# Last token block of a gated attention and convolution mix projected group by group from SBUF, its last group of heads normalized by 32x32 transposes on VectorE

## The chip, the cores and the metric

The kernel runs on one core of a Trainium2 chip. The core has five engines with an instruction queue each: TensorE (PE; its weight loads are listed as PEld), VectorE (DVE), ScalarE (ACT), GpSimd (POOL) and SyncE (SP), which here mostly issues DMAs. PE multiplies tiles held in SBUF and writes to PSUM, which has eight banks of 512 float32 columns on 128 partitions. The metric is the device time of one execution in microseconds, as a median of several runs. One more execution was recorded by the hardware profiler; all rows of a profile are of that one.

## What is computed

One batch of S = 2048 tokens, D = 640 channels, in bfloat16. `x = A_q` feeds two branches, and a gate of each token mixes them:

```python
x = A_q
g = _sigmoid((x * gate_w).sum(-1, keepdims=True))
a = _A_ref(x, A_k, A_v, A_shift_k, A_ssm_k, A_ssm_D)   # short shift, long convolution, times q
b = _B_ref(x, B_wq, B_wk, B_wv, B_wo)                  # attention
return g * a + (1 - g) * b

# _B_ref: 32 heads of Dh = 20, one shared k and v (multi-query)
q = (x @ wq).reshape(B, S, 32, 20).transpose(0, 2, 1, 3)
k = x @ wk
v = x @ wv
p = _softmax(einsum("bhqd,bkd->bhqk", q, k) * 20 ** -0.5)
o = einsum("bhqk,bkd->bhqd", p, v)
b = o.transpose(0, 2, 1, 3).reshape(B, S, 640) @ wo
```

The change is in the last two lines of the attention branch: the division of the softmax by its sum, and the product with `wo`, for the last quarter of the tokens.

## The kernel before

The tokens are cut into four blocks of 512 (`NB = 4`, index I). The 32 heads are cut into eight groups of four (index g); a head takes 32 of the 128 partitions, of which 20 hold its channels. For one block and one group the kernel walks over 16 tiles of 128 keys (index j). So `attention` (L879) has 4 x 8 x 16 = 512 steps u, 128 to a block. A step is: four matmuls QK (L893) into four PSUM banks, two exponentials of 128x1024 on ScalarE (L909; two steps in sixteen have one of them done by VectorE instead, L923 to L931), and four matmuls PV (L935) that add into bank 6. `vaug` carries a column of ones at position 20, so that row 20 of each head's 32 rows in bank 6 is the sum of the exponentials.

After the sixteen steps of a group `norm` (L990) divides. It copies bank 6 to `acc` (L994). The four rows of sums go by DMA to a 128x16 tile `den`, VectorE takes the reciprocal (L998), a DMA stores it to DRAM (`scr_d`), a DMA reads it back spread over all partitions (`rbc`), VectorE multiplies (L1004) into `oTn`, and a DMA stores that to DRAM (`scr_o`).

When all eight groups of a block are in `scr_o`, `oproj` (L1196) loads them in another layout (`oTp`, five tiles of 128 channels without the gaps), by four DMAs, and projects: for each of four tiles of 128 tokens (ci) and two halves of 320 output columns, five matmuls (L1211) and one eviction on VectorE (L1214), which scales by 1 - g (`omgf`) and adds the convolution branch, `kv`. The tile `outsb` is then stored to the output. `load_wo` (L1220) loads `wo` in the matching layout.

The convolution branch (`conv`, L1065) has its matmuls on PE, its spectra on VectorE and its complex products on GpSimd; it runs beside the attention and ends before the last block does.

Every operation is a node of a graph with the tiles that it reads and writes as keys. The `Scheduler` (L133) plays the graph through with modelled costs and writes out one fixed order for each engine. Three of its rules matter here. Operations marked `main` (QK, the exponentials, PV) keep their order, and the other matmuls come in groups, each with a PSUM bank, that are put in gaps of the main order by priority. A bank that a main operation uses is claimed for good (`bank_claimed`), and no group may take it afterwards. Where PE has nothing else and has been busy less than half of the last 2.4 modelled microseconds, a filler matmul with zero weights goes into bank 6 (L1256 names where it is made; not between the last PV of a group and the first of the next). On the chip each engine follows its list in order, with semaphore waits where another engine's result is needed. DMAs use one of 40 lanes, each with a semaphore; at the end SP waits for every lane in turn (L434 and L435).

`alloc` (L539) lays out SBUF: `xT` (x transposed, 20 KB a partition) and `wq_pad` (10 KB) are last read by the query projection of the last block (L839). `fence` (L127) makes the first writer of a family of tiles wait for all users of the families that lay there before. L502 is the helper through which all DMAs go.

Of the kernel before, what the change touches and what calls it, by code (L numbers as in the profile page):

```python
# [7 lines left out]
ALU = mybir.AluOpType  # L8
AX = mybir.AxisListType

BF16 = dt.bfloat16
F32 = dt.float32
# [120 lines left out]
class Scheduler:  # L133
# [238 lines left out]
    def emit(self, nc):  # L372
        def ctr(o):
            return "d%d" % o.lane if o.kind == "d" else "c_" + o.eng

        for op in self.linear:
            drop = [d for d in op.deps if op.eng == "pe" and d.eng == "pe" and d.kind == "c"]
            for d in drop:
                op.deps.discard(d)
            for d in op.deps:  # L380
                d.sig = True
        for e in ENGS:
            n = 0
            for op in self.order[e]:
                if op.kind == "d":
                    op.sig = True
                elif op.sig:
                    n += 1
                    op.value = n
        known = {e: {} for e in ENGS}  # L390
        waits = {}
        for op in self.linear:
            kn = known[op.eng]
            need = {}
            for d in sorted(op.deps, key=lambda o: -(o.value or 0)):
                c = ctr(d)
                if kn.get(c, 0) >= d.value:
                    continue
                if need.get(c, (0, None))[0] < d.value:
                    need[c] = (d.value, d)  # L400
            final = []
            items = sorted(need.items(), key=lambda kv: -kv[1][1].end)
            for c, (v, d) in items:
                if kn.get(c, 0) >= v:
                    continue
                final.append((c, v))
                for kc, kv in d.known.items():
                    if kn.get(kc, 0) < kv:
                        kn[kc] = kv
                kn[c] = max(kn.get(c, 0), v)  # L410
            waits[op] = final
            op.known = dict(kn) if op.sig else None
        lanes = [l for l in range(NLANES) if self.lanes[l]]
        names = ["c_" + e for e in ENGS] + ["d%d" % l for l in lanes]
        sems = {}
        cms = []
        for n in names:
            cm = nc.semaphore(n)
            sems[n] = cm.__enter__()
            cms.append(cm)  # L420
        bcm = nc.Block()
        block = bcm.__enter__()
        getter = {"sp": block.sync, "act": block.scalar, "pe": block.tensor, "dve": block.vector,
                  "pool": block.gpsimd}
        for e in ENGS:
            def body(eng, e=e):
                for op in self.order[e]:
                    for c, v in waits[op]:
                        eng.wait_ge(sems[c], v)
                    ins = op.fn(eng)  # L430
                    if op.sig:
                        ins.then_inc(sems[ctr(op)], 16 if op.kind == "d" else 1)
                if e == "sp":
                    for l in lanes:  # L434
                        eng.wait_ge(sems["d%d" % l], 16 * len(self.lanes[l]))  # L435
# [11 lines left out]
HD = 320  # L447
# [13 lines left out]
def c_ps(n):  # L461
    return 0.16 + 1.04e-3 * n
# [10 lines left out]
def c_pool(n):  # L473
    return 0.21 + 1.78e-3 * n


def c_mm(n):
    return 0.005 + 0.417e-3 * n


class Kernel:
# [57 lines left out]
    def alloc(self):  # L539
# [83 lines left out]
        last = [("wo", [128, NDC, D], BF16), ("oTp0", [128, NDC, 512], BF16), ("oTp1", [128, NDC, 512], BF16)]  # L623
        last += [(f"outsb{i}", [128, D], BF16) for i in range(4)]
        region("R2", keep + early0, keep + early, spec + late, last)
        self.fam0 = [n for n, _, _ in early0]
        self.early_fams = ["kslab", "vslab", "w4"] + [n for n, _, _ in early + keep]
        self.late_fams = ["AB", "X", "K", "Pp", "ssm_kT", "kst"]
# [250 lines left out]
    def attention(self, I):  # L879
# [105 lines left out]
                QK(u + 1, (2, 3))  # L985
        if hi == N:
            PV(N - 1)
            self.norm(NB - 1, 7)

    def norm(self, I, g):  # L990
        T = self.T
        k = I * 8 + g
        p = -900.0
        self.dve(lambda e: e.tensor_copy(T["acc"][:, :], self.bank(6)), [("ps", 6)], ["acc"], c_ps(512), prio=-9000.0,  # L994
                 name="acc")
        self.dma(T["den"][:, :], T["acc"][20:128:32, :].rearrange("r (a b) -> r a b", b=16), reads=["acc"],
                 writes=["den"], nbytes=8192, prio=p, name="den")
        self.dve(lambda e: e.reciprocal(T["rcp"][:, :], T["den"][:, :]), ["den"], ["rcp"], 0.3, prio=p, name="rcp")  # L998
# [5 lines left out]
        self.dve(lambda e: e.tensor_tensor(T["oTn"][:, :], T["acc"][:, :], T["rbc"][:, :], ALU.mult), ["acc", "rbc"],  # L1004
                 ["oTn"], c_ps(512), prio=p, port=True, name="onorm")
# [190 lines left out]
    def oproj(self, I):  # L1196
        T = self.T
        op = T[f"oTp{I % 2}"]
        so = self.scr_o[I].rearrange("(h d) c -> h d c", d=32)
        pr = 640.0 + 60.0 * I  # L1200
        for dd in range(4):
            self.dma(op[32 * dd:32 * dd + 32, :, :], so[:, dd:20:4, :], reads=[("scr_o", I, g) for g in range(8)],
                     writes=[("oTp", I % 2)], nbytes=163840, prio=-800, name="ld_oT")
        for ci in range(4):
            i = 4 * I + ci
            osb = T[f"outsb{i % 4}"]
            for half in range(2):
                n0 = HD * half
                gr = self.group("op", pr + ci, banks=(7,) if I < 3 else (7, 6, 5, 4, 3, 2, 1, 0))
                for kc in range(NDC):  # L1210
                    self.mm(gr, lambda e, bk, kc=kc, ci=ci, n0=n0: e.matmul(  # L1211
                        self.bank(bk, HD), op[:, kc, 128 * ci:128 * ci + 128], T["wo"][:, kc, n0:n0 + HD],
                        start=(kc == 0), stop=(kc == NDC - 1)), [("oTp", I % 2), "wo"], c_mm(HD))
                self.evac(gr, "dve", lambda e, bk, osb=osb, n0=n0, i=i: e.scalar_tensor_tensor(  # L1214
                    osb[:, n0:n0 + HD], self.bank(bk, HD), T["omgf"][:, i:i + 1], T["kv"][:, i, n0:n0 + HD],
                    ALU.mult, ALU.add), ["omgf", ("A", i)], [("outsb", i % 4)], c_ps(HD))
            self.dma(self.aps["out"][0][128 * i:128 * i + 128, :], osb[:, :], reads=[("outsb", i % 4)],
                     nbytes=163840, prio=-800, name="st_out")
# [92 lines left out]
```

## Time and profile before

| what | us |
|---|---|
| median of 3 runs (985.41 to 987.27) | 985.71 |
| the profiled execution | 980.84 |
| its span, first to last instruction | 979.0 |
| PE, VectorE, ScalarE, GpSimd busy | 817.0, 621.8, 914.0, 370.2 |
| mean granted PE clock, of full speed | 0.964 |

The page cuts the span into 40 slices of 24.5 us and gives the busy share of an engine in each as a digit (9 is 90% or more), the granted clock of PE, and the DMA load:

```profile
PE   6687777988999989998889998989998898878814
DVE  8669862476765776568877576566766666654501
ACT  7499999999999999999999999999999999999920
POOL 2370000787434287243682352772447800000000
PEclk9899999999999999999999999999999899998775
```

The last two slices, from 930 us on, differ from the rest: ScalarE has a 2 and a 0 there.

In the rows of groups of instructions, the line is that of the code, then engine, operation, tile written and tiles read, partitions x elements with the type, the count, busy us and mean ns of one, and the idle time before them with what ended it. Rows of the chain have start, length and what ran. Rows of a single line or tile give minimum, median and maximum in ns and the first and last start.

### The profile page before, as it was taken

The page shows a single profiled execution, that of the slowest core. Times are in us where ns is not written, and L with a number is a line of the kernel's source. Part 1 is how long each engine was busy: PE and PEld are TensorE (multiplying, and loading weights), DVE is VectorE, ACT ScalarE, POOL GpSimd, SP SyncE. Part 2 cuts the span into 40 slices and gives each one's busy share as a digit, 9 for nine tenths or more (in the row PEclk, how much of TensorE's full clock was granted, in tenths as well). Part 3 has the DMA queues.
Part 4 walks back from the last instruction along what each step waited for, and adds up shares of the span by engine and source line. Part 5 has one row for each costly group of instructions (what it writes and reads, how often), then busy time and mean ns, then how long its engine had stood idle before and what let it go on. Part 6 is the DMA issues. An engine that isn't in the chain of part 4 may idle for free.

```text
span 979.0 us, 16386 instructions
## 1 busy us (share of the span) xinstructions
PE 817.0 (83%) x6892; PEld 338.0 (35%) x6892; DVE 621.8 (64%) x819; ACT 914.0 (93%) x1004; POOL 370.2 (38%) x307
## 2 busy tenths in 40 slices
PE   6687777988999989998889998989998898878814
PEld 4222113443444334442433443444443243322101
DVE  8669862476765776568877576566766666654501
ACT  7499999999999999999999999999999999999920
POOL 2370000787434287243682352772447800000000
PEclk9899999999999999999999999999999899998775
DMA  5415611001000000000010000000000031110001
GB/s 150 150 47 177 211 56 29 13 18 40 18 18 18 18 30 14 15 18 18 19 40 18 18 13 9 16 17 18 17 18 18 18 99 59 53 37 18 17 31 40
DMA packets 35136, 40.39 MB, mean 41 GB/s; under 512 B 13436, under 2 KB 28278, under 8 KB 35062
## 3 DMA queue, kind: packets, MB, share of 16 engines
q1 hardware_dynamic: 32438, 39.09, 12.7%
q8 instruction: 54, 0.88, 0.4%
q10 hardware_dynamic: 2624, 0.26, 0.2%
q14 instruction: 20, 0.16, 0.1%
HBM read 31.86 MB, written 7.08 MB: 40 GB/s over the span
## 4 chain that ended last, share of the span: by engine, by line
ACT 86%; PE 6%; DMA 4%; DVE 3%; issue 0%; ACTq 0%
ACT ET L909 86%; PE ps L893 1%; PE ps L1211 1%; DMA rbc<-scr_d 1%; DMA oTp<-scr_o 1%; PE ps L1256 1%; PE ps L935 1%; DMA qT<-cr 1%; PE ps L839 1%; PE ps L1113 1%; PE ps L768 0%; DMA xn<-in_A_q_dram 0%; DVE outsb L1214 0%; DMA scr_d<-rcp 0%; DVE sq L845 0%
## 5 line engine op out<-in xcount | busy, mean ns | idle before, releaser
L909 ACT ACTIVATE ET<-ps 128x1024 bf16<-128x1024 f32 x970 | 891.0, 1182 | 11.6 <-PE ps L893 11.3
L893 PE MATMUL ps<-qT,kT 21*128 21x512 bf16 x2048 | 225.6, 390 | 112.0 <-ACT ET L909 102.2
L1144 POOL TENSOR_TENSOR Pp<-X,K 128x512 f32<-128x512 bf16 x120 | 170.5, 1446 | 361.3 <-DVE K L1132 361.0
L935 PE MATMUL ps<-ET,vaug 128*32 128x512 bf16 x1940 | 209.0, 393 | 1.0 <-ACT ET L909 1.0
L893 PEld LDWEIGHTS ps<-qT,kT 21*128 21x128 bf16 x2048 | 56.3, 91 | 281.2 <-ACT ET L909 266.4
L935 PEld LDWEIGHTS ps<-ET,vaug 128*32 128x32 bf16 x1940 | 52.3, 93 | 118.0 <-issue 113.4
L923 DVE TENSOR_SCALAR dJ<-ps 128x1024 uint32<-128x1024 f32 x54 | 66.0, 1222 | 41.1 <-PE ps L893 40.8
L1256 PE MATMUL ps<-Tcos,zeros 128*128 128x512 bf16 x262 | 83.5, 403 | 0.0
L1144 POOL TENSOR_TENSOR AB<-Pp 128x256 bf16<-128x256 f32 x80 | 79.3, 991 | 6.0
L931 DVE SCALAR_TENSOR_TENSOR ETd<-dJ,dE 128x1024 bf16<-128x1024 f32 x54 | 79.7, 1476 | 1.1
L928 DVE SCALAR_TENSOR_TENSOR dE<-dJ,dE 128x1024 f32<-128x1024 uint16 x54 | 79.4, 1471 | 0.7
L1177 PE MATMUL ps<-AB,Tcos 128*128 128x256 bf16 x320 | 76.4, 275 | 0.8 <-DVE K L1132 0.6
L930 DVE SCALAR_TENSOR_TENSOR dJ<-dJ 128x1024 f32<-128x1024 uint16 x54 | 74.6, 1381 | 0.7
L1177 PE MATMUL ps<-AB,Tsin 128*128 128x256 bf16 x280 | 67.2, 273 | 0.0
L994 DVE COPY acc<-ps 128x512 f32<-128x512 f32 x32 | 22.1, 692 | 62.9 <-PE ps L935 62.4
L1144 POOL TENSOR_TENSOR Pp<-Pp 128x512 f32<-128x512 f32 x40 | 60.6, 1515 | 3.1
L1004 DVE TENSOR_TENSOR oTn<-acc,rbc 128x512 bf16<-128x512 f32 x32 | 29.2, 912 | 45.2 <-DMA rbc<-scr_d 45.1
L1211 PE MATMUL ps<-wo,oTp 128*128 128x320 bf16 x160 | 34.1, 344 | 26.2 <-DMA oTp<-scr_o 21.2
L1113 PE MATMUL ps<-ssm_kT,Tsin 128*128 128x256 bf16 x320 | 49.5, 274 | 0.0
L1124 DVE TENSOR_SCALAR X<-ps 128x512 bf16<-128x512 f32 x35 | 24.1, 687 | 39.6 <-PE ps L1113 39.5
L1113 PE MATMUL ps<-kv,Tcos 128*128 128x256 bf16 x320 | 47.4, 275 | 1.1 <-DVE K L1132 0.9
L1130 DVE CAST K<-ps 128x256 bf16<-128x256 f32 x40 | 16.9, 422 | 49.4 <-PE ps L1113 49.1
(118 smaller groups left out, 796.1 us busy)
## 6 DMA issues: line engine op xcount, KB each, us to landing
kslab<-in_A_k_dram SPq DMA_DIRECT2D x15, 640.0 KB, 4.0
rbc<-scr_d SPq DMA_DIRECT2D x32, 256.0 KB
scr_o<-oTn SPq DMA_DIRECT2D x32, 128.0 KB, 1.8
xn<-in_A_q_dram SPq DMA_DIRECT2D x4, 640.0 KB
vslab<-in_A_v_dram SPq DMA_DIRECT2D x16, 160.0 KB, 3.3
kst<-in_A_ssm_k_dram SPq DMA_DIRECT2D x5, 512.0 KB, 3.6
oTp<-scr_o SPq DMA_DIRECT2D x16, 160.0 KB, 2.4
out_dram<-outsb SPq DMA_DIRECT2D x16, 160.0 KB, 1.8
```

What stands on the lines that cost most here:

```text
L893: o = op("pe", lambda e, r=r, Iu=Iu, g=g, j=j, bk=banks[r]: e.matmul(self.bank(bk), T["kT4"][32 * r:32 * r + 21, 128 * j:128 * j + 128], T ...
L909: op("act", lambda e, p=p, slot=slot: e.activation(T[f"ET{slot}"][:, :], self.ps[:, 1024 * p:1024 * p + 1024], ACT.Exp, scale=SCALE), [("p ...
L923: V(lambda e, p=p: e.tensor_scalar(J[:, :], self.ps[:, 1024 * p:1024 * p + 1024], SCALE * LOG2E * 65536.0, EOFF * 65536.0, ALU.mult, ALU.add),
L928: V(lambda e: e.scalar_tensor_tensor(Ef, lo, ED, Ef, ALU.add, ALU.mult), [kJ, "dE"], ["dE"], c_ps(1024), **k)
L930: V(lambda e: e.scalar_tensor_tensor(Jf, lo, EP, lo, ALU.add, ALU.mult), [kJ], [kJ], c_ps(1024), **k)
L931: V(lambda e: e.scalar_tensor_tensor(T["ETd"][:, :], Jf, EQ, Ef, ALU.add, ALU.mult), [kJ, "dE"], ["ETd"], c_ps(1024), **k)
L935: return op("pe", lambda e, r=r, j=j, src=src: e.matmul(self.bank(6)[32 * r:32 * r + 32, :], T["vaug"][:, j, :], src[:, 512 * (r % 2):512 ...
L1113: o = self.mm(gr, lambda e, bk, lhs=lhs, rhs=rhs, comp=comp, n=n: e.matmul(self.bank(bk, 256, 256 * comp), lhs, rhs, start=(n == 0), stop= ...
L1144: f = lambda e: e.tensor_tensor(out, a, b, alu)
L1177: self.mm(gr, lambda e, bk, lhs=lhs, fc=fc, comp=comp, h=h: e.matmul(self.bank(bk, 256, 256 * h), lhs, AB[:, fc, :, comp, :], start=(fc == ...
L1211: self.mm(gr, lambda e, bk, kc=kc, ci=ci, n0=n0: e.matmul(self.bank(bk, HD), op[:, kc, 128 * ci:128 * ci + 128], T["wo"][:, kc, n0:n0 + HD ...
L1256: sch.filler = lambda e: e.matmul(self.bank(6), self.T["zeros"][:, :], self.T["Tcos"][:, 0, 0:512], start=False, stop=False)
```

## The change

For the last block (I = 3) nothing goes through DRAM any more between `norm` and the projection, and the projection is made by groups of heads.

- `norm` of groups 0 to 6 of the last block multiplies into `oT3[:, g, :]` in SBUF instead of `oTn`, and does not store it; its three small DMAs stay.
- `load_wog` loads `wo` a second time, by groups: 128 partitions, of which each head's 20 carry rows of `wo` and the others zeros. Eight memsets on GpSimd and four DMAs. `oT3` and `part` lie over `xT`, `wog` over `wq_pad`, with fences.
- `part` projects groups 0 to 5: for each ci and half six matmuls (op1) on bank 7 and an eviction that scales, adds `kv` and writes `part` in float32.
- `tail` takes group 7 after the last PV: a VectorE transpose in blocks of 32x32 from bank 6, which brings the sums of the exponentials into columns, a reciprocal of 128x16, a product, and a second transpose into `oT3[:, 7, :]`. Group 6's product (op2) opens all eight banks, with six warm-up matmuls of zero weights behind each of the last two token tiles; group 7's product closes them. One eviction for each ci covers both halves (two banks). The four stores alternate between the SP and the ACT queue. All of these matmuls are `main`.
- `oproj` runs for the first three blocks only. SP's closing waits are sorted by the planned end of each lane's last DMA.

```diff
                 if e == "sp":
-                    for l in lanes:
+                    for l in sorted(lanes, key=lambda l: self.lanes[l][-1].end):
                         eng.wait_ge(sems["d%d" % l], 16 * len(self.lanes[l]))
...
+        over("oT3", "xT", 0, [128, 8, 512], BF16)
+        over("part", "xT", 8192, [128, 4, D], F32)
+        over("wog", "wq_pad", 0, [128, 8, D], BF16)
...
             PV(N - 1)
-            self.norm(NB - 1, 7)
...
-        self.dve(lambda e: e.tensor_tensor(T["oTn"][:, :], T["acc"][:, :], T["rbc"][:, :], ALU.mult), ["acc", "rbc"],
-                 ["oTn"], c_ps(512), prio=p, port=True, name="onorm")
-        self.dma(self.scr_o[I][128 * g:128 * g + 128, :], T["oTn"][:, :], reads=["oTn"], writes=[("scr_o", I, g)],
-                 nbytes=131072, prio=p, name="o_st")
+        out, key = (T["oT3"][:, g, :], ("oT3", g)) if last else (T["oTn"][:, :], "oTn")
+        self.dve(lambda e: e.tensor_tensor(out, T["acc"][:, :], T["rbc"][:, :], ALU.mult), ["acc", "rbc"],
+                 [key], c_ps(512), prio=p, port=True, name="onorm")
+        if not last:
+            self.dma(self.scr_o[I][128 * g:128 * g + 128, :], T["oTn"][:, :], reads=["oTn"], writes=[("scr_o", I, g)],
+                     nbytes=131072, prio=p, name="o_st")
+
+    def load_wog(self):
+        w = self.aps["B_wo"].rearrange("(g r d) n -> r d g n", r=4, d=20)
+        for g in range(8):
+            self.pool(lambda e, g=g: e.memset(T["wog"][:, g, :], 0.0), (), ["wog"], c_pool(320), prio=700, name="wog0")
+        for r in range(4):
+            self.dma(T["wog"][32 * r:32 * r + 20, :, :], w[r], reads=(), writes=["wog"], nbytes=204800, prio=700,
+                     name="ld_wog")
+
+    def part(self):
+        for ci in range(4):
+            for half in range(2):
+                n0 = HD * half
+                gr = self.group("op1", 900.0 + ci)
+                for g in range(6):
+                    self.mm(gr, lambda e, bk, g=g, ci=ci, n0=n0: e.matmul(
+                        self.bank(bk, HD), T["oT3"][:, g, 128 * ci:128 * ci + 128], T["wog"][:, g, n0:n0 + HD],
+                        start=(g == 0), stop=(g == 5)), [("oT3", g), "wog"], c_mm(HD))
+                self.evac(gr, "dve", lambda e, bk, ci=ci, n0=n0, i=i: e.scalar_tensor_tensor(
+                    T["part"][:, ci, n0:n0 + HD], self.bank(bk, HD), T["omgf"][:, i:i + 1], T["kv"][:, i, n0:n0 + HD],
+                    ALU.mult, ALU.add), ["omgf", ("A", i)], [("part", ci)], c_ps(HD))
+
+    def tail(self):
+        acc, g = T["acc"], 7
+        v = lambda t: t[:, :].rearrange("p (b r) -> p b r", r=32)
+        self.dve(lambda e: e.transpose(acc[:, :], self.bank(6)), [("ps", 6)], ["acc"], c_ps(512), prio=p, name="tp")
+        self.dve(lambda e: e.reciprocal(T["rcp"][:, :], v(acc)[:, :, 20]), ["acc"], ["rcp"], 0.3, prio=p, name="rcp")
+        self.dve(lambda e: e.tensor_tensor(v(T["oTn"]), v(acc), T["rcp"][:, :].unsqueeze(2).to_broadcast([128, 16, 32]),
+                                           ALU.mult), ["acc", "rcp"], ["oTn"], c_ps(512), prio=p, port=True,
+                 name="onorm")
+        self.dve(lambda e: e.transpose(T["oT3"][:, g, :], T["oTn"][:, :]), ["oTn"], [("oT3", g)], c_ps(512), prio=p,
+                 name="tp")
...
+        for ci in range(4):
+            for half in range(2):
+                mm(ci, half, 6)
+            if ci >= 2:
+                for _ in range(6):
+                    warm()
+        for ci in range(4):
+            for half in range(2):
+                mm(ci, half, 7)
+            self.dve(lambda e, ci=ci, i=i, osb=osb: e.scalar_tensor_tensor(
+                osb[:, :].rearrange("p (h n) -> p h n", h=2),
+                self.ps[:, 1024 * ci:1024 * ci + 1024].rearrange("p (h n) -> p h n", h=2)[:, :, 0:HD],
+                T["omgf"][:, i:i + 1], T["part"][:, ci, :].rearrange("p (h n) -> p h n", h=2), ALU.mult, ALU.add),
+                ["omgf", ("ps", 2 * ci), ("ps", 2 * ci + 1), ("part", ci)], [("outsb", ci)], c_ps(D), prio=p,
+                name="op2_ev")
+            self.dma(self.aps["out"][0][128 * i:128 * i + 128, :], osb[:, :], reads=[("outsb", ci)],
+                     nbytes=163840, prio=p, name="st_out", eng="act" if ci % 2 else "sp")
...
         for I in range(NB):
+            if I == NB - 1:
+                self.g.fence(["oT3", "part"], ["xT"])
+                self.g.fence(["wog"], ["wq_pad"])
+                self.load_wog()
             self.attention(I)
...
-        for I in range(NB):
+        for I in range(NB - 1):
             self.oproj(I)
+        self.part()
+        self.tail()
```

More of the change, by code (lines that the diff above doesn't have):

```diff
@@ L625, in alloc, with over @@
         region("R2", keep + early0, keep + early, spec + late, last)
+        def over(name, under, off, shape, dtype):
+            T[name] = nc.alloc_sbuf_tensor_at(name, shape, dtype, offset=nc.lookup_mloc(T[under]).addr + off)
+        over("oT3", "xT", 0, [128, 8, 512], BF16)
+        over("part", "xT", 8192, [128, 4, D], F32)
+        over("wog", "wq_pad", 0, [128, 8, D], BF16)
         self.fam0 = [n for n, _, _ in early0]
@@ L995, in norm @@
                  name="acc")
+        last = I == NB - 1
         self.dma(T["den"][:, :], T["acc"][20:128:32, :].rearrange("r (a b) -> r a b", b=16), reads=["acc"],
@@ new lines, in norm @@
+        self.dve(lambda e: e.tensor_tensor(out, T["acc"][:, :], T["rbc"][:, :], ALU.mult), ["acc", "rbc"],
[4 more added lines that the diff above has]
+    def load_wog(self):
+        T = self.T
+        w = self.aps["B_wo"].rearrange("(g r d) n -> r d g n", r=4, d=20)
[4 more added lines that the diff above has]
+                     name="ld_wog")
@@ new lines, in part @@
+    def part(self):
+        T = self.T
+        for ci in range(4):
[6 more added lines that the diff above has]
+                        start=(g == 0), stop=(g == 5)), [("oT3", g), "wog"], c_mm(HD))
+                i = 4 * (NB - 1) + ci
+                self.evac(gr, "dve", lambda e, bk, ci=ci, n0=n0, i=i: e.scalar_tensor_tensor(
+                    T["part"][:, ci, n0:n0 + HD], self.bank(bk, HD), T["omgf"][:, i:i + 1], T["kv"][:, i, n0:n0 + HD],
+                    ALU.mult, ALU.add), ["omgf", ("A", i)], [("part", ci)], c_ps(HD))
@@ new lines, in tail, with mm, warm @@
+    def tail(self):
+        T = self.T
+        acc, g = T["acc"], 7
+        v = lambda t: t[:, :].rearrange("p (b r) -> p b r", r=32)
+        p = -9000.0
+        self.dve(lambda e: e.transpose(acc[:, :], self.bank(6)), [("ps", 6)], ["acc"], c_ps(512), prio=p, name="tp")
[5 more added lines that the diff above has]
+                 name="tp")
+        def mm(ci, half, g):
+            b, n0 = 2 * ci + half, HD * half
+            self.op("pe", lambda e: e.matmul(
+                self.bank(b, HD), T["oT3"][:, g, 128 * ci:128 * ci + 128], T["wog"][:, g, n0:n0 + HD],
+                start=(g == 6), stop=(g == 7)), [("oT3", g), "wog"], [("ps", b)], c_mm(HD), name="op2", main=True,
+                banks=(b,))
+        def warm():
+            self.op("pe", lambda e: e.matmul(self.bank(0, HD), T["zeros"][:, :], T["wog"][:, 6, 0:HD], start=False,
+                                             stop=False), ["zeros", "wog"], [("ps", 0)], c_mm(HD), name="warm",
+                    main=True, banks=(0,))
+        for ci in range(4):
[5 more added lines that the diff above has]
+        for ci in range(4):
+            i = 4 * (NB - 1) + ci
+            osb = T[f"outsb{ci}"]
+            for half in range(2):
[8 more added lines that the diff above has]
+                     nbytes=163840, prio=p, name="st_out", eng="act" if ci % 2 else "sp")
@@ L1208, in oproj @@
                 n0 = HD * half
-                gr = self.group("op", pr + ci, banks=(7,) if I < 3 else (7, 6, 5, 4, 3, 2, 1, 0))
+                gr = self.group("op", pr + ci, banks=(7,))
                 for kc in range(NDC):
```

## The prediction

> **What bounds the kernel now.** I read the page first, then the chain of waits from 925 us on, then windows over the last 240 us, then single rows for prices.
>
> ```profile
> span 979.0 us, 16386 instructions
> L909 ACT ACTIVATE ET<-ps 128x1024 bf16<-128x1024 f32 x970 | 891.0, 1182 | 11.6 <-PE ps L893 11.3
> ```
>
> ScalarE's exponentials fill 891.0 us of 979.0. They are the bound until the last of them; nothing in the change makes one cheaper. What is left is the end of the chain (start, length, what):
>
> ```profile
> 936.99 0.41 PE ps L935 x2
> 937.42 0.70 DVE acc L994
> ...
> 938.14 1.85 DMA den<-acc
> ...
> 940.02 0.27 DVE rcp L998
> ...
> 940.30 1.38 DMA scr_d<-rcp
> ...
> 941.71 4.73 DMA rbc<-scr_d
> ...
> 946.45 0.70 DVE oTn L1004
> ...
> 947.17 1.70 DMA scr_o<-oTn
> ...
> 948.88 2.45 DMA oTp<-scr_o
> ...
> 956.23 2.33 DMA oTp<-scr_o
> ...
> 958.61 1.53 PE ps L1211 x5
> ...
> 960.77 1.53 PE ps L1211 x5
> ...
> 975.28 0.55 DVE outsb L1214
> ```
>
> The last product with V is out at 937.40. From there to 979.00 run 41.6 us in which one thing at a time happens: nine DMA legs one behind the other up to 958.56, eight rounds of five matmuls and one eviction (2.16 us each, 960.77 - 958.61, all on bank 7, because the planner has given banks 0 to 6 to attention) up to 975.83, and 3.17 us after that. The last piece:
>
> ```profile
> DMA to landing us min/median/max: 1.8/1.8/1.8
> SPq L435 <- DMA out_dram<-outsb: 1.2, 1, 1.2
> L435 SPq EVENT_SEMAPHORE  x20: 17/28/28, 976.2 to 978.6; - x20
> ```
>
> The last store, issued at 975.86, lands 1.8 us later, near 977.66. SP's closing waits run until 978.6 although only 1.2 us of their 2.4 us was a wait for that store: the other 1.2 us are 20 instructions, some 0.06 us each, and most of them stand behind the wait for the last store. 0.4 us of closing follow.
>
> **The change part by part.** All sums are against the profiled execution's span (979.0 us; its own time is 980.84, 1.84 around it). The median shown is 985.71, 4.87 above that; I let this difference stand as it is.
>
> *Tail on VectorE.* Everything from 937.42 to 958.56 goes; in its place stand a transpose of 512 columns out of PSUM, a reciprocal of 16 columns, a product of 512 columns and a second transpose in bf16. The reciprocal is the chain's 0.27 and the product its 0.70 (GpSimd is idle there, as it will be). No transpose on VectorE is in the trace; the nearest rows:
>
> ```profile
> L994 DVE COPY acc<-ps 128x512 f32<-128x512 f32 x32 | 22.1, 692 | 62.9 <-PE ps L935 62.4
> L535 DVE COPY xT<-ps 128x512 bf16<-128x512 bf16 x7 | 2.9, 419 | 0.3 <-ACT xT L536 0.3
> L923 DVE TENSOR_SCALAR dJ<-ps 128x1024 uint32<-128x1024 f32 x54 | 66.0, 1222 | 41.1 <-PE ps L893 40.8
> L1214 DVE SCALAR_TENSOR_TENSOR outsb<-ps,omgf,kv 128x320 bf16<-128x320 f32 x32 | 17.6, 550 | 35.1 <-PE ps L1211 34.7
> ```
>
> Below, the packed copy, 0.42; above, every element taken twice, 1.22 (the 1024 columns of L923). I take the plain copy of the same tile, 0.69, for each. So oT3 of group 7 is there at 937.42 + 0.69 + 0.27 + 0.70 + 0.69 and three hand-overs of 0.02 (937.42 against 936.99 + 0.41): **939.83**. The two ends give 939.3 and 940.9.
>
> [...]
>
> *Closing matmuls.* PE meanwhile runs eight op2 matmuls of group 6 and twelve warm-up matmuls, then for each of four token tiles two of group 7. Prices of 320-column matmuls at full clock, and the clock (seventh item of a window row after the engines' counts is the granted clock):
>
> ```profile
> 852.72 0.85 PE L1211 MATMUL ps<-wo,oTp 128*128 128x320 bf16 x5
> 855.58 0.45 PE L1211 MATMUL ps<-wo,oTp 128*128 128x320 bf16 x2
> 939.00:940.00 1.00, 0.00 (x0) 0.00 (x0) 0.00 (x0) 0.00 (x0) 0.00 (x0) 0.98 0.07 8
> 940.00:941.00 1.00, 0.00 (x0) 0.00 (x0) 0.26 (x1) 0.00 (x0) 0.00 (x0) 0.50 0.00 0
> ```
>
> One more matmul costs 0.40/3 = 0.13 to 0.14 us. Twenty, streaming from about 937.25, are through at 940.0: the warm-ups outlast oT3 by some 0.15 us. A pair takes 0.45 with its drain, so the first eviction starts at **940.47**. In the profile the mean of 0.98 says that the clock fell only at 939.96, after 2.5 idle microseconds; with PE busy in that stretch I take full clock.
>
> *Four evictions.* Each now covers both halves, 640 columns out of two banks: 0.55 for 320 and 320 more at (1222 - 692)/512 = 1.035 ns make 0.88. Four with 0.03 between them: 3.61, to **944.08**. PE makes a pair in 0.27, so VectorE sets this pace. Before, the same work was eight rounds, 17.3 us.
>
> *Stores and closing waits.* 0.02 and 1.8 to landing (944.08 to 945.90). ci 1 and 3 go out on ACT's queue, which has been idle since the last exponential; the trace has no late DMA there, so from 0 to 0.5 more, and I take 0. The closing waits are now sorted by planned end, so that what stands behind the last store's landing is one wait and the 0.4 us: 0.45 instead of 979.0 - 977.66 = 1.34. If the order changes nothing, 0.9 comes back.
>
> *Sum:* the span ends at 944.08 + 0.02 + 1.80 + 0.45 = **946.35**, 32.65 us earlier. The profiled execution would take 948.2; the timed median **953.1**.
>
> *What moves ahead.* Instead of 40 matmuls after the end, 48 (op1, groups 0 to 5) and eight evictions come before it. They need group 5, whose normalization ends near 891.4:
>
> ```profile
> L994 DVE COPY acc<-ps x3: 691/691/692, 880.4 to 937.4; 128x512 f32<-128x512 f32 x3
> L1004 DVE TENSOR_TENSOR oTn<-acc,rbc x3: 691/691/693, 890.7 to 946.5; 128x512 bf16<-128x512 f32 x3
> 909.47 0.69 DVE L994 COPY acc<-ps 128x512 f32<-128x512 f32 x1 [8.35 <-PE ps L935]
> ```
>
> (The first two rows are group 5 to group 7, first and last start; the third is group 6.) So op1 has 891 to 937. Their cover is measured: the first three blocks' projection lay in the same kind of stage. Engine windows (PE, PEld, DVE, ACT, POOL, clock), then L1211's own part of the first:
>
> ```profile
> 840.00:860.00 20.00, 17.50 (x142) 6.41 (x138) 14.78 (x21) 20.00 (x23) 0.00 (x0) 1.00 0.13 43
> 880.00:900.00 20.00, 15.96 (x106) 3.76 (x102) 11.48 (x13) 18.77 (x21) 0.00 (x0) 0.83 0.07 22
> 900.00:920.00 20.00, 15.91 (x106) 3.90 (x102) 7.86 (x9) 19.11 (x22) 0.00 (x0) 0.82 0.05 15
> 920.00:937.00 17.00, 13.11 (x95) 3.14 (x94) 5.87 (x6) 16.35 (x18) 0.00 (x0) 0.92 0.03 9
> 840.00:860.00 20.00, 8.78 (x48) 3.79 (x48) 1.00 0.13 43
> ```
>
> Exactly 48 projection matmuls ran in 840 to 860, and ACT was busy 20.00 of 20. After 880 PE carries filler instead:
>
> ```profile
> 880.00:900.00 20.00, 6.31 (x16) 1.29 (x16) 0.83 0.07 22
> 900.00:920.00 20.00, 6.97 (x20) 1.69 (x20) 0.82 0.05 15
> 920.00:937.00 17.00, 4.91 (x15) 0.97 (x14) 0.92 0.03 9
> ```
>
> These are L1256's rows of the same windows; the planner adds filler only where nothing else runs, so op1 takes its place. I cost op1 at nothing. Bounds: ACT stands idle for 1.23 + 0.89 + 0.65 = 2.77 us in these windows, and their mean clock is 0.83, 0.82 and 0.92; if real work cures that, 2.8 comes on top. Against: one more such dip is 1.4. And op1 is a new wait of PE for group 5; behind it in PE's order stand the next QK, and behind those ACT. The chain from acc to oTn took 10.3 us there but 9.0 in the quiet end, so a plan that expects it quick stalls by up to 1.3. Together -2.8 to +2.7.
>
> *Loads.* wog needs eight GpSimd memsets and four DMAs on SP, after the last read of wq_pad:
>
> ```profile
> L839 PE MATMUL ps<-xT,wq_pad x160: 379/379/631, 16.0 to 523.6; 128*128 128x512 bf16 x160
> L675 POOL MEMSET wk<- 128x640 bf16 x1 | 0.6, 631 | 0.0
> 550.00:600.00 50.00, 45.79 (x407) 20.86 (x407) 35.09 (x41) 50.00 (x56) 17.20 (x13) 1.00 0.06 17
> ```
>
> 8 x 0.63 = 5.0 us on an engine that is free for 33 of those 50 us, long before op1: nothing. oT3 in SBUF drops seven more stores of oTn from SP; they were hidden, so nothing. What is late next is group 6's normalization: it started 27.9 us before the end, is done after 10 or 11, and has 17 us to spare.
>
> **The rivals.** (1) *The clock halves at the end.* The planner puts no filler between a group's last PV and the next group's first, and the two windows with the low clock, 880 to 920, are those with a group end in them (880.4, 909.5). At half clock five matmuls take 1.53 instead of 0.85: twenty queued ones 2.75 more, the first pair 0.27 more, so 3.0 later: **956.1**. Against it: the clock held until 939.96 with PE idle. [...]
>
> (2) *op1 is not hidden*, because its groups find no gap and end up at or behind the last exponential. A round is then 0.85 + 0.14 + 0.55 + 0.08 (the hand-overs: 2.16 - 1.53 - 0.55 = 0.08) = 1.6, eight are 12.9: up to **966**. The window with 48 matmuls speaks against it.
>
> (3) *SP stands behind the wog loads.* They wait on SP, in order, for the memsets, which queue on GpSimd behind the convolution's products; the den, rcp and rbc transfers queue behind them, and the next group cannot empty bank 6 until oTn is done, so PV, QK and ACT stop. A group lasts 29.1 us (880.4 to 909.5) and its normalization 11: ACT feels it only from 18 us of delay on, and from 18 + 32.7 = 51 us on the kernel is **slower, over 985.7**; 60 us would give 995. With 33 free of 50 us on GpSimd that is improbable.
>
> (4) *The change does not do what it says*: the end still waits for a DMA, were group 6's path late by its 17 us and 20 more. Then nearly nothing is gained, **about 985**.
>
> **How the numbers follow.** Forecast 0.78, clock 0.08, op1 exposed 0.08, a mixture of small losses beyond the range 0.02, SP 0.03, no effect 0.01. Unknown terms about 953.1: stage -2.8 to +2.7, transposes -0.5 to +1.1, ACT's queue up to +0.5, closing waits up to +0.9. All at once are improbable; -3.1 and +4.4 take in most of it, and rival 1: **950.0 to 957.5**. A measurement of this kernel tells about 0.2%, 2 us, from no change. Faster 0.96, same 0.01, slower 0.03.
>
> **What would show it.** Right: after the last PV a VectorE chain of four operations of 2.3 to 2.4 us; four evictions of 0.88; the span ending some 2.3 us behind the last of them; ACT's busy share from 880 on no lower than before; op1 between 891 and 937. Wrong: a transpose of 1.2 us or more, a clock of 0.50 at 938, an op1 group behind the last exponential, or ACT idle before QK at about 891 with PE waiting for oT3.

## The result and the profile after

| | before | after |
|---|---|---|
| median of 4 runs, us | 985.56 (984.09 to 987.27) | 949.27 (948.80 to 955.80) |
| ratio, 95% interval | | 0.9647 (0.9602 to 0.9691) |
| span of the first record, us | 979.0 | 947.7 |
| from VectorE's first operation behind the last PV to the end | 41.6 (from 937.42) | 8.7 (from 939.00) |
| mean granted PE clock | 0.964 | 0.981 |

The forecast was 953.1, in a range of 950.0 to 957.5. The direction was right, and the gain was 36.3 us where 32.6 were forecast, so that the measured median lies 0.7 us under the range. In the experiments below, one execution of experiment 6 (2242.38 us) and one of experiment 10 (3602.9 us) have no known cause and are left out of all figures. The head of the page after, and its row of exponentials:

```profile
span 947.7 us, 16341 instructions
PE 798.1 (84%) x6843; PEld 338.4 (36%) x6903; DVE 623.8 (66%) x824; ACT 914.2 (96%) x1004; POOL 375.0 (40%) x315
L915 ACT ACTIVATE ET<-ps 128x1024 bf16<-128x1024 f32 x970 | 891.2, 1201 | 12.9 <-PE ps L899 12.4
```

The exponentials are as they were (891.2 us against 891.0, idle 12.9 against 11.6); what went is time behind them. The end as a timeline of VectorE (start, length, operation), with ACT's stores:

```profile
939.00 0.72 DVE L1049 STREAM_TRANSPOSE acc<-ps 128x512 f32<-128x512 f32 x1 [7.01 <-PE ps L941]
939.75 0.25 DVE L1050 RECIPROCAL rcp<-acc 128x16 f32<-128x16 f32 x1
940.04 0.69 DVE L1051 TENSOR_TENSOR oTn<-acc,rcp 128x512 bf16<-128x512 f32 x1
940.76 0.71 DVE L1054 STREAM_TRANSPOSE oT<-oTn 128x512 bf16<-128x512 bf16 x1
942.09 3.26 DVE L1081 SCALAR_TENSOR_TENSOR outsb<-ps,omgf,part 128x640 bf16<-128x640 f32 x4 [0.61 <-PE ps L1059]
943.79 1.95 ACTq L502 DMA_DIRECT2D out_dram<-outsb  x2
```

The eight DMA legs of the chain (the prediction counts nine; its sum goes by their end and does not use the count), with the copy, reciprocal and product between them, are now 2.47 us of VectorE, and eight rounds of matmul and eviction are four evictions in 3.26 us. op1, wog and SP's closing waits by their lines (ns minimum, median, maximum; first and last start), then the clock in windows:

```profile
L1035 PE MATMUL ps<-wog,oT x48: 299/299/310, 896.0 to 913.3; 128*128 128x320 bf16 x48
L1022 POOL MEMSET wog<- x8: 631/631/1134, 525.6 to 530.9; 128x640 bf16 x8
L502 SPq DMA_DIRECT2D wog<-in_B_wo_dram x4: 282/336/465, 534.6 to 545.6; - x4
L435 SPq EVENT_SEMAPHORE  x20: 17/28/28, 945.0 to 947.2; - x20
896.00:914.00 18.00, 15.76 (x133) 6.14 (x132) 10.16 (x14) 18.00 (x21) 0.00 (x0) 1.00 0.00 1
937.00:942.00 5.00, 3.95 (x29) 2.45 (x28) 2.37 (x4) 1.51 (x2) 0.00 (x0) 1.00 0.00 0
```

While op1 ran, ACT was busy 18.00 of 18 us; in the tail the clock stayed at 1.00 and fell only near 946.2, 3.3 us behind the last matmul.

### The profile page after: what moved, and what is told of

The parts are those of the page before. It is cut to its first block, busy times and chain, and to the rows that moved or that the text cites. A ratio compares the mean times of both kernels' runs of the same rounds, so it can differ in the third digit from the quotient of the medians.

```text
span 947.7 us, 16341 instructions
## 1 busy us (share of the span) xinstructions
PE 798.1 (84%) x6843; PEld 338.4 (36%) x6903; DVE 623.8 (66%) x824; ACT 914.2 (96%) x1004; POOL 375.0 (40%) x315
## 4 chain that ended last, share of the span: by engine, by line
ACT 91%; PE 6%; DVE 2%; DMA 1%; issue 0%; DVEq 0%
ACT ET L915 90%; PE ps L899 1%; PE ps L941 1%; PE ps L1343 1%; DMA qT<-cr 1%; PE ps L845 1%; PE ps L1258 1%; DMA xn<-in_A_q_dram 1%; PE ps L774 0%; PE ps L1059 0%; PE ps L787 0%; DVE tprod L717 0%; DVE outsb L1081 0%; PE ps L1066 0%; ACT xT L536 0%
## 5 line engine op out<-in xcount | busy, mean ns | idle before, releaser
L915 ACT ACTIVATE ET<-ps 128x1024 bf16<-128x1024 f32 x970 | 891.2, 1201 | 12.9 <-PE ps L899 12.4
L1225 POOL TENSOR_TENSOR Pp<-X,K 128x512 f32<-128x512 bf16 x120 | 172.6, 1464 | 349.2 <-DVE K L1213 348.9
L1225 POOL TENSOR_TENSOR AB<-Pp 128x256 bf16<-128x256 f32 x80 | 74.5, 931 | 6.0
L1343 PE MATMUL ps<-Tcos,zeros 128*128 128x512 bf16 x187 | 59.8, 402 | 5.0 <-issue 5.0
L1194 PE MATMUL ps<-kv,Tsin 128*128 128x256 bf16 x320 | 47.1, 274 | 0.0
L1194 PE MATMUL ps<-ssm_kT,Tcos 128*128 128x256 bf16 x320 | 44.8, 274 | 1.5 <-DVE X L1205 0.6
```

The source lines that it names most:

```text
L915: op("act", lambda e, p=p, slot=slot: e.activation(T[f"ET{slot}"][:, :], self.ps[:, 1024 * p:1024 * p + 1024], ACT.Exp, scale=SCALE), [("p ...
L1194: o = self.mm(gr, lambda e, bk, lhs=lhs, rhs=rhs, comp=comp, n=n: e.matmul(self.bank(bk, 256, 256 * comp), lhs, rhs, start=(n == 0), stop= ...
L1225: f = lambda e: e.tensor_tensor(out, a, b, alu)
```

## The experiments

The tail of each is taken from its own record, from VectorE's first operation behind the last PV to the end of the span. That separates it from the attention stage, whose length varies. "Half clock" is (1 - mean clock) x 2 x span of a run, the time that PE would have spent at half speed.

**1. The kernel before once more.** No edit.

> The kernel before, unchanged, recorded once more: its first record (span 979.0 us) lies 4 to 6 us below its own timed runs, the changed kernel's does not. Theory A (chance): the attention stage of either kernel loses a few microseconds to stretches of halved clock, more or fewer from one execution to the next; the first record had few. Then this record has a last PV some 3 to 6 us later than 937.4, with more stretches of clock 0.5 before it, and the same 41.6 us behind the last PV; and the timed runs of both kernels scatter by 5 us. Rival B: the records of the kernel before are always short (recording itself changes it): then this one is 979 to 981 again, while its timed runs stay at 984 to 987. Rival C: the tail is longer in the timed runs; not visible in a record, but then the recorded tail would have to vary too: it would differ from 41.6 by over 1 us.

983.47 us, median of 12 (981.25 to 987.59); the kernel before beside it 985.62 (17 runs, 980.49 to 988.36). Over these 29 runs the span is 961.4 + 0.25 x half clock, with a correlation of 0.94: 980.5 us goes with a clock of 0.964, 988.4 with 0.949. Two theories have a part in it. The stage of the record ended 3.3 us later than 937.42 (A), and its tail was not the same 41.6 us but 2.8 us shorter, which is C's sign: the tail varies too. VectorE's timeline of the record:

```profile
940.68 0.69 DVE L994 COPY acc<-ps 128x512 f32<-128x512 f32 x1 [7.36 <-PE ps L935]
...
969.70 0.55 DVE L1214 SCALAR_TENSOR_TENSOR outsb<-ps,omgf,kv 128x320 bf16<-128x320 f32 x1 [1.61 <-PE ps L1211]
971.20 0.55 DVE L1214 SCALAR_TENSOR_TENSOR outsb<-ps,omgf,kv 128x320 bf16<-128x320 f32 x1 [0.95 <-PE ps L1211]
```

The same record in windows (seventh entry: PE clock):

```profile
964.00:968.00 4.00, 2.86 (x10) 1.04 (x8) 1.01 (x2) 0.00 (x0) 0.00 (x0) 0.50 0.12 41
968.00:972.00 4.00, 2.56 (x12) 1.15 (x13) 1.20 (x3) 0.00 (x0) 0.00 (x0) 0.81 0.12 41
972.00:976.00 4.00, 2.37 (x15) 1.06 (x13) 1.40 (x3) 0.00 (x0) 0.00 (x0) 1.00 0.12 41
```

In the middle of the old projection the clock came back to 1.00, and the last four rounds took 1.50 us instead of 2.16. Rival B is not needed, because runs as short as the two records, 980.49 and 980.89 us, stand among the timed ones; it is not excluded either, because this record, 981.25 us, is again the shortest of its twelve executions, and its span of 979.5 us is what B forecast. The records of experiments 10 and 11, kernels of the same family, are the second shortest of eleven and the shortest of four.

**2. No warm-ups.**

```diff
-                for _ in range(6):
+                for _ in range(0):
                     warm()
```

> The changed kernel without the twelve warm-up matmuls (they add zero to bank 0). Theory: the clock holds for some 2.5 us of idle PE after the last PV anyway, and the warm-ups end after oT3 is ready; without them the first closing eviction starts 0.1 to 0.2 us earlier and the tail (last PV to end of span) goes from 8.7 to about 8.6 us. Rival (clock gate): without them PE has 1.1 us of matmuls in the 2.5 us that VectorE needs, the clock falls to 0.5 before group 7's matmuls, their first pair takes 0.72 instead of 0.45 us, and the tail is 8.9 us or more. Either way the time moves by less than 0.5 us.

The tail is 8.65 us (from 937.15 to 945.8), 0.05 less. The first eviction started 3.02 us behind the first transpose instead of 3.09. The time, 947.57 us (947.40 to 950.38), lies inside the scatter of the changed kernel and cannot show so little. The clock did not fall, though PE was busy for only a third of two microseconds (windows of this record):

```profile
938.00:939.00 1.00, 0.37 (x3) 0.04 (x2) 0.93 (x3) 0.00 (x0) 0.00 (x0) 1.00 0.00 0
939.00:940.00 1.00, 0.31 (x3) 0.24 (x4) 0.63 (x1) 0.00 (x0) 0.00 (x0) 1.00 0.00 0
```

So in this record the warm-ups keep nothing up that would fall, and neither this experiment's rival nor rival 1 of the prediction showed. One record cannot say how often it would.

**3. Closing waits in the order of the lanes.**

```diff
-                    for l in sorted(lanes, key=lambda l: self.lanes[l][-1].end):
+                    for l in lanes:
```

> The changed kernel with SP's closing waits in the order of the lanes, as before the change. Theory: most of the twenty wait instructions (0.06 us each) then stand behind the landing of the last store, and the span ends 3.0 to 3.3 us behind the last eviction instead of 2.35: tail 9.4 to 9.7 us. Rival: the waits are passed while the stores fly, because the last lanes happen to stand last: tail 8.7 us as it is.

The tail is 9.40 us, 0.70 more, which is the theory's lower end. SP stood 1.79 us in one wait, and waits that would have been passed earlier came behind it. The row of the waits:

```profile
L435 SPq EVENT_SEMAPHORE  x20: 17/28/1790, 943.2 to 946.1; - x20
```

The time itself (949.63, 945.93 to 950.99) cannot show 0.7 us.

**4. Group 7 through DRAM.** In `tail`, `self.norm(NB - 1, 7)` in place of the four VectorE operations.

> The changed kernel, but group 7 is normalized as before the change (copy, three DMAs through DRAM, product) instead of by two transposes; all else stays. Theory (transposes buy the DMA legs and no more): from the last PV to the end of the product 9.75 us as in the kernel before, against 2.5; the clock is at half by then, so the first pair takes 0.72 instead of 0.45 us; tail 8.7 + 7.3 + 0.1 = 16.1 us, time about 7.4 us above the changed kernel. Rival: the DMAs of this part were slow only because they stood alone at the end in the old order (or are faster or slower next to the new tail): tail differs from 16.1 by over 1 us.

The time is 957.47 us and the tail 16.27, as forecast. It takes 9.2 us from the copy to the start of the product, and group 7's eight matmuls run at half clock, 2.31 us instead of 1.25. From its timeline:

```profile
939.43 0.69 DVE L999 COPY acc<-ps 128x512 f32<-128x512 f32 x1 [7.93 <-PE ps L941]
...
948.59 0.69 DVE L1011 TENSOR_TENSOR oT<-acc,rbc 128x512 bf16<-128x512 f32 x1 [6.34 <-DMA rbc<-scr_d]
949.34 2.31 PE L1053 MATMUL ps<-wog,oT 128*128 128x320 bf16 x8 [7.13 <-DVE oT L1011]
```

The transposes are worth 7.6 us of the 32.9 by which the tail became shorter.

**5. The changed kernel again.** No edit.

> The changed kernel unchanged, for its scatter. Over 29 runs of the kernel before, the span follows the time that PE spent at half clock, (1 - mean clock) x 2 x span: a line of 0.25 us of span for 1 us at half clock. Some 39 us of the 85 in the mean lie in the old tail; 46 in the stage before the last PV. Theory T1 (chance): the stage of the changed kernel is the same, some 46 us at half clock in the mean, and the four runs so far (30 to 63) were few. T2: the change also thins the half-clock time of the stage (op1 instead of filler, or another planned order): 30 to 40 us in the mean of these runs and a median of 947.5 to 950.

949.42 us (945.56 to 953.51), ratio 0.9653 (0.9610 to 0.9695) to the kernel before run beside it. Half clock 38.2 us in the mean, as T2 had it; span = 938.4 + 0.25 x half clock over all ten runs of the changed kernel. Whether op1 or the order does it, experiments 6 and 10 tell.

**6. op1 behind the end.**

```diff
-                start=(g == 6), stop=(g == 7))
+                start=(g == 0), stop=(g == 7))
...
-                mm(ci, half, 6)
-            if ci >= 2:
-                for _ in range(6):
-                    warm()
+                for h in range(7):
+                    mm(ci, half, h)
...
-        self.part()
```

> The changed kernel with groups 0 to 5 projected behind the last PV too, each bank's seven matmuls in a row where op2 of group 6 and the warm-ups stood; the eviction adds kv as before, and the eight op1 evictions are gone. 56 matmuls of 0.1375 us are 7.7 us on PE while VectorE needs 2.5: the first eviction starts 8.0 us behind the last PV instead of 3.1, tail 13.6 to 13.8 us instead of 8.7. If op1 was hidden at nothing: time 4.9 us above the changed kernel's. If op1 in the stage costs ACT something: less than 4.9. If op1 is what thins the half-clock time (T2 by op1): the stage goes back to some 46 us at half clock, and the time is 7 to 8 us above. If only another planned order does: 4.9.

The time is 955.10 us (952.55 to 957.48) beside 949.42, and the tail 13.58, 4.9 more, as worked out. The medians differ by 5.7, which the scatter of five and six runs cannot tell from 4.9. PE streams 64 matmuls in 8.87 us and VectorE waits 5.5, as the timeline has them:

```profile
942.00 8.87 PE L1059 MATMUL ps<-wog,oT 128*128 128x320 bf16 x64
...
950.10 3.26 DVE L1079 SCALAR_TENSOR_TENSOR outsb<-ps,omgf,kv 128x640 bf16<-128x640 f32 x4 [5.50 <-PE ps L1059]
```

Half clock stays at 39.7 us in the mean. op1 in the stage costs ACT nothing that shows, and it is not what thins the half-clock time.

**7. More filler.** `FILL = 0.7` instead of 0.5.

> The changed kernel with the planner's bound for filler matmuls at 0.7 busy instead of 0.5. Theory: the half-clock time in the stage comes from stretches in which PE is busy 50 to 70% by plan and the clock gate counts that as idle; then it falls below 15 us and the time by 0.25 us for each, some 5 us: 943 to 946. Rival 1: the gate trips at the ends of groups, where no filler may stand; then nothing changes, 949. Rival 2: more filler stands ahead of QK in PE's order and ACT waits for it: slower than 949 with a higher clock.

949.36 us (947.00 to 953.66): the same as 949.42, with half clock down from 38.2 to 26.3 us. On the line of experiment 5 that should have been worth 3 us. The theory's 943 to 946 is missed; rival 1 has the time but not the lower half clock, rival 2 the half clock but not the time. That half-busy stretches count as idle for the clock was the author's guess: it fits the fall at 912.65 in the first record, behind 3.41 us in which PE was busy for 2.30, but a bound was not shown. That filler in PE's in-order list takes back what the clock gives would fit, but it is not shown: no row here says where it stands in the way. It may also be that half clock goes with a long span without being what costs the time.

**8. ScalarE takes two of the closing evictions.**

```diff
-                    T["part"][:, ci, n0:n0 + HD], self.bank(bk, HD), T["omgf"][:, i:i + 1], T["kv"][:, i, n0:n0 + HD],
+                    T["part"][:, ci, n0:n0 + HD], T["kv"][:, i, n0:n0 + HD], T["romgf"][:, i:i + 1], self.bank(bk, HD),
...
+                mm(ci, half, -1)
                 mm(ci, half, 6)
...
+            if ci % 2:
+                self.op("act", lambda e, dst=dst, src=src, i=i: e.activation(dst, src, ACT.Copy,
+                                                                             scale=T["omgf"][:, i:i + 1]),
...
+                self.dve(lambda e, dst=dst, src=src, i=i: e.tensor_scalar(dst, src, T["omgf"][:, i:i + 1], None, ALU.mult),
...
```

> The changed kernel with the convolution branch and groups 0 to 5 added by an identity matmul in PSUM (kept in bf16, divided by 1 - g) instead of at the eviction, so that the closing evictions are a scaling and ScalarE, idle there, takes two of the four; the eight identity matmuls stand where the twelve warm-ups stood. The four evictions of 3.3 us become two beside two: the last ends 1.5 us earlier, tail 7.2 us instead of 8.7, time 1.5 us less. Rival: ScalarE's first instruction of another function loads a table (over 1 us) or its 640 columns cost more than 0.9 us: tail 8 us or more.

`mm(ci, half, -1)` is the identity matmul. The closing evictions in the timeline:

```profile
940.83 1.68 DVE L1085 TENSOR_SCALAR outsb<-ps,omgf 128x640 bf16<-128x640 f32 x2 [0.54 <-PE ps L1065]
941.11 1.48 ACT L1081 ACTIVATE outsb<-ps,omgf 128x640 bf16<-128x640 f32 x2 [3.78 <-PE ps L1065]
```

948.09 us (947.21 to 950.67), ratio 0.9643 (0.9601 to 0.9686); tail 7.58, 1.1 less. The evictions lost 1.5 us as forecast, but from the last of them to the end it is 2.8 us instead of 2.35. The stores now come close together: all four are issued from 941.75 to 942.98, while in the changed kernel's record they came 0.8 us apart and the 16 DMA engines were busy for 0.61 of the time from 944.0 to 946.8. That the stores delay each other is what fits; it was not tried by itself. No table load shows among ACT's rows behind the last PV (the first record has three in all, of 1.28 us each). It has the shortest tail of the study; by its times it cannot be told from the changed kernel (949.42, run beside it).

**9. Closing evictions in halves**, one of 320 columns for each bank.

> The changed kernel with its closing evictions in halves: eight of 320 columns out of one bank instead of four of 640 out of two. 8 x 0.55 and seven hand-overs of 0.03 are 4.6 us instead of 3.3, and the first starts 0.14 us earlier: tail 9.9 us instead of 8.7. Rival: VectorE overlaps neighbouring evictions (the four of 0.88 took 3.26, not 3.52), so that eight cost 0.47 each: tail 9.2 us.

VectorE's timeline:

```profile
948.29 3.76 DVE L1083 SCALAR_TENSOR_TENSOR outsb<-ps,omgf,part 128x320 bf16<-128x320 f32 x8 [0.48 <-PE ps L1059]
```

The tail is 9.06, 0.36 more: nearer to the rival's 9.2 than to the theory's 9.9. Eight pass in 3.76 us, 0.47 each, where one alone is listed with 0.55. Covering two banks with one eviction saves 0.5 us on VectorE and 0.36 in the tail. (One execution, 956.21 us, in a stage that ended at 945.3.)

**10. The kernel before with the loads of wog alone**, unused.

```diff
+            if I == NB - 1:
+                self.g.fence(["wog"], ["wq_pad"])
+                self.load_wog()
             self.attention(I)
```

> The kernel before with nothing added but the loads of wog (memsets and DMAs, unused). Its planned order on PE is that of the changed kernel up to op1 (2217 rows from the start), and so differs from the kernel before from about 524 us on. T3 (the other order is what thins the half-clock time of the stage): mean of the runs 2 to 3 us under that of the kernel before in the same call, with some 10 us less at half clock (74 instead of 84). T1 (the two kernels' stages differ by chance only): the same mean within 1 us and 84 us at half clock. Tail as before, 38 to 42 us.

981.76 us (977.64 to 986.18) beside 984.84 for the kernel before: ratio 0.9976 (0.9955 to 0.9997). In the mean 981.7 against 984.3, half clock 72.2 against 84.6 us, as T3 forecast. The record's tail is 41.3. The traces bear out the order: PE's weight loads come in the same order here and in the changed kernel up to op1, and here and in experiment 6 up to the last PV, while those of the kernel before differ from 531 us on. So the kernel became 2.6 us shorter (with a standard error of 1; the interval of the ratio leaves 0.3 to 4.4) by twelve unneeded operations from 524 us on. They can hardly help by themselves, so the planner's other order is the likely cause; no run has one without the other. Which stretch of it keeps the clock up is open: single records of the two orders scatter more than they differ.

**11. The kernel before, last projection on all eight banks.**

```diff
-                gr = self.group("op", pr + ci, banks=(7,) if I < 3 else (7, 6, 5, 4, 3, 2, 1, 0))
+                if I == NB - 1:
+                    b = 2 * ci + half
...
+                            name="op", main=True, banks=(b,))
```

> The kernel before with the last block's 40 matmuls on all eight banks in a row, evictions as before; normalization and DRAM trip as before. PE then does not wait for evictions: 40 matmuls at half clock are 40 x 0.275 = 11.0 us, and the last eviction follows: 11.8 us instead of 17.3 from the landing of the last load, 5.5 us less; tail 36.1 instead of 41.6 in a record whose clock stays at half, and 1 to 2 us less still where the clock comes back after some 3.4 us of work. Rival: evictions or stores bound the rounds and it gains under 3 us.

The time is 977.51 us, ratio 0.9923 (0.9896 to 0.9951), and the tail 33.0 us. That is 8.6 less than the first record's 41.6, more than either theory had, but 5.8 less than the 38.8 of experiment 1, in whose old projection the clock came back. In the mean of the runs it is 6.7 us (977.6 against 984.3). VectorE's timeline:

```profile
964.27 0.55 DVE L1216 SCALAR_TENSOR_TENSOR outsb<-ps,omgf,kv 128x320 bf16<-128x320 f32 x1 [0.78 <-PE ps L1212]
...
965.61 0.55 DVE L1216 SCALAR_TENSOR_TENSOR outsb<-ps,omgf,kv 128x320 bf16<-128x320 f32 x1 [0.78 <-PE ps L1212]
966.57 3.27 DVE L1216 SCALAR_TENSOR_TENSOR outsb<-ps,omgf,kv 128x320 bf16<-128x320 f32 x5 [0.41 <-PE ps L1212]
```

Windows of the same record:

```profile
960.00:965.00 5.00, 3.61 (x14) 2.04 (x15) 1.10 (x2) 0.00 (x0) 0.00 (x0) 0.50 0.10 32
965.00:970.00 5.00, 4.25 (x28) 2.64 (x25) 3.31 (x6) 0.00 (x0) 0.00 (x0) 0.90 0.28 98
```

PE is dense here (busy for 3.61 us of the 3.61 from its first matmul, at 961.39, to 965.0), the clock returned after 4.6 us (near 966.0), and from 966.6 on evictions follow each other. That some 3.4 us of work bring the clock back was not shown here; the record of experiment 1 has one such stretch, 3.5 us at half clock (a mean of 0.93 in the 25 us from 360 on). The 40 matmuls so take 7.86 us instead of the 11.0 worked out at half clock. That the waits for one bank cost twice, themselves and the clock, would fit: the first record's eight rounds ran at half clock to the end (0.50 in all windows from 960 on), those of experiment 1 only to the middle (0.50, then 0.81 and 1.00).

## Why the prediction was right, and where it was off

**VectorE's tail.** Forecast 2.41 us to oT3 (0.69, 0.27, 0.70, 0.69 and hand-overs), measured 2.47 (0.72, 0.25, 0.69, 0.71). The choice of the plain copy as the price of a transpose was right in float32 and in bf16, and bf16 gained nothing from its size.

**Closing matmuls and evictions.** First eviction forecast 3.05 us behind the first transpose's start, measured 3.09; four evictions 3.61, measured 3.26, because neighbouring ones overlap (start to start 0.79, listed 0.88). **Stores and closing waits:** 2.27 forecast, 2.35 measured, and experiment 3 shows that sorting is worth 0.7 of it, not 0.9. **Whole tail:** 8.9 forecast from 937.42, 8.7 measured.

**What moves ahead.** "I cost op1 at nothing" held: ACT 18.00 of 18 while op1 ran, and with op1 behind the end (experiment 6) the tail grows by 4.9 us and the half clock stays. The wait for group 5 did not show. None of the four rivals occurred: the clock did not halve before the closing matmuls, op1 ran from 896.0 to 913.6, and the last load of wog was issued at 545.6 us.

**What was wrong** is two terms outside the tail. First, "I let this difference stand as it is": the 4.87 us between the recorded execution and the median compare one execution with three, and executions scatter by more than that (979 to 991 us). Over 57 more runs of the kernel before the mean is 984.2, not 985.7: the base was 1.5 us too high. Whether recording itself shortens this kernel stays open (experiment 1). Second, "nothing" for the loads of wog: they cost nothing, but with them the order on PE changed from 531 us on, and experiment 10 was 2.6 us shorter. That size lay inside the stage's -2.8 to +2.7, but I had looked for it in op1: it lay there by luck. From 984.2, less 32.65 and 2.6, comes 949.0; the changed kernel's ten runs have a mean of 950.0. The rest is 1.0, the size of the error of these means, and on the side on which the old tail is: 41.6, 38.8 and 41.3 us in three records, so that the sum against 41.6 took a little too much. The first two records alone do not show the gain in the stage: there the changed kernel's last PV came 1.6 us later (939.00 against 937.42).

**Where the gain came from.** Of 32.9 us in the tail the transposes carry 7.6 (experiment 4), op1 ahead of the end 4.9 (experiment 6) and the sorted waits 0.7 (experiment 3). Eight banks alone gave 5.8 to 8.6 in the old order, by which record of the kernel before they are compared with (experiment 11; it overlaps with op1). The store of oTn and the reload of oTp, 11.4 us in the chain before, are gone; that part was not undone by itself.

## What to carry to other kernels

Once a bound engine has finished, read the chain behind it row by row: every leg there counts in full. Sums of measured rows hit the tail within 0.3 us here for the change itself and in experiments 2, 3, 4 and 6; they missed by 0.4 where stores came together (experiment 8), by 0.8 where evictions overlapped (experiment 9) and by more than 1 where the clock came back (experiment 11). Before a time of a few per mille is forecast, take several runs and their granted clock, not one record's distance to a median. And in a kernel with a planned order, even an unused operation moves that order: test it alone before a gain is credited to what was meant to bring it.

## What the runs showed of the hardware

- **The scatter goes with the clock.** Both kernels follow one slope: 0.25 to 0.26 us of span for each microsecond at half clock (57 and 10 runs, correlation 0.96 and 0.97), 979 to 991 us for the same program. That the clock is the cause is not shown: in experiment 7 the half clock fell by 12 us and the time stayed.
- **When the clock falls is not a matter of idle time alone.** 2.6 us without a matmul sufficed in the first record, from 937.40 to 939.96; in experiment 4 the clock still was 1.00 at the end of the window below, 2.8 us behind the last matmul. The stretches at half clock before the tail last 6.83 or 10.24 us in the first record and 10.24 or 13.65 in the changed kernel's, all multiples of 3.41, their difference. Nor was PE idle ahead of each fall: in the first record the clock fell at 881.93 behind 3.41 us in which PE was busy for 1.73, and at 912.65 behind 3.41 us in which it was busy for 2.30. The clock came back after 4.6 us of dense matmuls in experiment 11, after 8 us of rounds with gaps in experiment 1, and not at all in 16.7 us of the same rounds in the first record. The window of experiment 4:

```profile
943.00:945.00 2.00, 0.00 (x0) 0.00 (x0) 0.00 (x0) 0.00 (x0) 0.00 (x0) 1.00 0.05 4
```

- **Neighbouring evictions from PSUM overlap** by 0.08 us on VectorE: four listed with 0.88 pass in 3.26, eight listed with 0.54 to 0.55 in 3.76. Their rows in the changed kernel and in experiment 9 (ns minimum, median, maximum; first and last start):

```profile
L1081 DVE SCALAR_TENSOR_TENSOR outsb<-ps,omgf,part x4: 876/876/884, 942.1 to 944.5; 128x640 bf16<-128x640 f32 x4
L1083 DVE SCALAR_TENSOR_TENSOR outsb<-ps,omgf,part x8: 543/543/552, 948.3 to 951.5; 128x320 bf16<-128x320 f32 x8
```
